# Two of four output-row blocks of a convolution's first pointwise product, computed by seven block products instead of eight at the turn between query groups of a Conformer layer

## The chip, the cores and the metric

The kernel runs on one core of one Trainium2 chip. The metric is the device time of one execution in microseconds (us); lower is better. Shown are the median of three runs, and one execution taken by the hardware profiler, from which all durations come.

## The reference

The reference is one Conformer layer on x of shape [2, 4000, 512] in bfloat16, with normalisations over the 512 features:

```python
x1 = x  + 0.5 * silu(ln(x) @ w_ff1_a) @ w_ff1_b           # 512 -> 2048 -> 512
x2 = x1 + softmax(q k^T * scale) v @ w_o                   # q, k, v from ln(x1)
h  = ln(x2) @ w_pw1                                        # 512 -> 1024
h  = h[..., :512] * sigmoid(h[..., 512:])                  # gate
dc = depthwise convolution of h over time, three taps      # then a norm over all tokens
x3 = x2 + silu(norm(dc)) @ w_pw2
x4 = x3 + 0.5 * silu(ln(x3) @ w_ff2_a) @ w_ff2_b
return ln(x4)
```

The change concerns `ln(x2) @ w_pw1` and the gate behind it.

## The kernel before

**Chunks and groups.** Each of the two sequences is cut into eight chunks of 512 tokens (the last has 416), so there are 16 chunks, c or t = 0 to 15. The first feed-forward part runs over all chunks, then the attention, then the second feed-forward part. The attention (`attention`, L2050) runs over 16 query groups g, one per chunk, and in each over 32 tiles of 128 keys; the loop variable is kt = 0 to 31, called a step of the group here. Chunk g - 1 passes beside group g through everything that follows its attention: `units_late` finishes its product with the values in steps 0 to 6 of group g, projects it, and normalises it (`ln_beside`, L1127, temporaries `ltm`, then transposes into `lnT[0]`). From `lnT[0]` comes the first pointwise product.

**Scores and values by seven products.** In groups 1 to 7 and 9 to 15 the scores of key tiles 2 to 29 are computed by quads of four key tiles (`score_quad`, L1993): 2 x 2 blocks of keys and of queries, seven block products instead of eight (the Strassen-Winograd scheme), every matmul with 256 columns (208 in the narrow groups). A quad takes four steps. It uses the PSUM banks s0 (called c), s1 (x) and s2 (h). Product 5 goes to h and is copied by ScalarE to `m5s` in SBUF (the tile region xt); product 1 goes to c and is copied to h; product 6 accumulates onto h; VectorE adds h and m5 into x; product 2 accumulates onto c, which is then done; product 7 accumulates onto h, and VectorE adds h and m5 into m5; products 3 and 4 accumulate onto x and h. Exponentials follow on ScalarE. Groups 0 and 8 ("plain") compute all scores directly. Key tiles 0, 1 and 30 are direct in every group, with four matmuls of 512 columns, in steps 0, 1 and 30. The tail of 32 keys is done by `tail_scores` (L2232) in step 24 (21 in group 0), in bank s1. The product with the values likewise takes seven products per pair of key tiles (`pv`), in banks y0 to y3 and s3, and is joined by VectorE in `pv_join` at the turn to the next group. The sums of the softmax (`pair_sums`, `sum_plain`, `sum_tail`, `split_sums`) are VectorE's too.

**The first pointwise product.** For chunk t, `pw1` (L2405) computes one block of 128 output rows by four matmuls of 512 columns. `conv_b` (L2361) takes a block of the gate's half and ScalarE computes its tanh into `th`; `conv_a` (L2372) takes the matching block of the other half and VectorE multiplies: (tanh + 1) times the PSUM bank, into `G`. A pair of the two, `pair(t, jj)` (L2733), serves block jj of four. Pairs 0 and 1 of chunk t come in steps 24 and 28 of group t + 1, in banks s0 and s1, and pairs 2 and 3 in steps 3 and 5 of group t + 2, in banks y1 and y3 (`att_hook`, L2741). Then GpSimd copies the one-column halos, and `taps_beside` (L2423) applies the three taps with ScalarE and VectorE.

**What sets the order.** The recorded operations are put in order by a planner (`Plan`, `once` at L272). It works from a table of instruction costs, moves matmuls ahead of each other within 8 us of the recorded order, and gives each engine its instructions in the order in which its model would start them; so a change moves neighbours too. SyncE issues nearly all DMAs in such an order: the streams of key and value forms (`kfd`, `v12d`), transposes, and stores. A DMA that waits at the head of the queue holds back what is behind it.

**Where things lie.** Region "work" holds `lnT[0]`, `lnT[1]` and `ltm`; `lnT[1]` also holds the next queries (`lin`), `last7` (L860), in which the last pair sums are kept, and the transposed sums `sT`. Region "wff" holds the weights `Wp1` and the gate's buffers. All recorded instructions carry line L93 in the profile, so operations are told apart by the regions they write and read, as in `s<-work,wff`: a PSUM bank s from work and wff.

Of the kernel before, what the change touches and what calls it, by code (L numbers as in the profile page):

```python
# [17 lines left out]
CHUNK = TPC * TILE  # L18
# [532 lines left out]
class Conformer:  # L551
# [35 lines left out]
    def memory(self):  # L587
# [269 lines left out]
        self.m3 = C.view(oP + (self.NP - 1) * 1024, CHUNK, parts=3)  # L857
        self.b_m3 = [C.buf("m3", oP + (self.NP - 1) * 1024 + j * 2 * TILE, 2 * TILE) for j in range(TPC)]

        self.last7, self.b_last7 = C.view(oLT + 4096, CHUNK), C.buf("last7", oLT + 4096, 2 * CHUNK)  # L860
        self.hl = C.view(oHL, 1024).rearrange("p (h c k) -> p h c k", h=2, c=DC)
        self.sT = C.view(oLT + 6144, 1024).rearrange("p (h c k) -> p h c k", h=2, c=DC)
        self.b_sT = [C.buf("sT", oLT + 6144 + h * 1024, 1024) for h in range(2)]
# [932 lines left out]
    def pair_sums(self, g, j, step):  # L1796

        S, s, W = self.S, g % TCB % 2, width(g)
        hw = W // 2
        i, n = self.group(j)[0], len(self.group(j))  # L1800
        r, m, ft, b_f = self.p_home(g, i)
        at = (i + 1) % 2
        R = self.Rt[:, r:r + n, :, 0:hw]
        a12, a22 = R[:, :, 0], R[:, :, 1]
        a11, a21 = [t[:, m:m + n, 0:hw] for t in self.Tt]
        b_11, b_21 = [b[m:m + n] for b in self.b_T]
        b_12, b_22 = self.b_R[r:r + n], self.b_R2[r:r + n]
        s4, s1, s2 = [ft[:, k, at:at + n, 0:hw] for k in range(3)]
        if step < 4:
            out, x, y, op, rd, wr = ((s1, a21, a22, ALU.add, b_21 + b_22, [b_f[1]]),  # L1810
                                     (s2, s1, a11, ALU.subtract, b_11 + [b_f[1]], [b_f[2]]),
                                     (a21, a11, a21, ALU.subtract, b_11 + b_21, b_21),
                                     (s4, a12, s2, ALU.subtract, b_12 + [b_f[2]], [b_f[0]]))[step]
            S.op("DVE", lambda e: e.tensor_tensor(out=out, in0=x, in1=y, op=op), reads=rd, writes=wr)
            return
        acc = self.acc[s][:, 0:W].rearrange("p (h k) -> p h k", h=2)
        if step == 6:
            S.op("DVE", lambda e: e.tensor_tensor(out=acc[:, 0], in0=acc[:, 0], in1=acc[:, 1], op=ALU.add),
                 reads=[self.b_acc[s]], writes=[self.b_acc[s]])
            return  # L1820
        if j == 0:
            return
        sig = [ft[:, 0:2, at + k, 0:hw] for k in range(n)]
        t, b_t = (self.P30, self.b_P30) if j < GROUPS - 1 else (self.last7, self.b_last7)
        two = t[:, 0:W].rearrange("p (h k) -> p h k", h=2)
        if step == 4:
            out, x, y, rd, wr = two, sig[0], sig[1], b_f[0:2], [b_t]
        elif j == 1:
            _, _, f0, b_0 = self.p_home(g, 0)
            out, x, y, rd, wr = acc, two, f0[:, 0:2, 1, 0:hw], [b_t] + b_0[0:2], [self.b_acc[s]]  # L1830
        else:
            out, x, y, rd, wr = acc, acc, two, [b_t, self.b_acc[s]], [self.b_acc[s]]
        S.op("DVE", lambda e: e.tensor_tensor(out=out, in0=x, in1=y, op=ALU.add), reads=rd, writes=wr)
# [216 lines left out]
    def attention(self, old, hook):  # L2050

        for g in range(NCK):
            W, plain = width(g), g % TCB == 0
            for kt in range(KT):
                if plain:
                    self.ring = [0, 1, 2]
                else:
                    self.ring, self.rings["S"] = list(self.ASIDE.get(kt, (0, 1))), 0
                if plain and kt < KT - 1 or kt < 2 or kt == KT - 2:
                    ps, b_ps = self.scores(g, kt, None if plain else self.bank((0, 2)[kt] if kt < 2 else 0))  # L2060
                    if kt < KT - 2:
                        self.exp_pair(g, kt, ps, b_ps)
                    else:
                        self.act(self.P30[:, 0:W], ps[:, 0:W], AF.Exp, [b_ps], [self.b_P30], scale=SCALE)
                elif not plain and kt < KT - 2:
                    self.score_quad(g, *divmod(kt - 2, 4))
                if g == 0 and kt < 2:
                    self.pop(old // 2 if kt == 0 else old - old // 2)
                if kt == (24 if g else 21):
                    self.tail_scores(g)  # L2070
                if g:
                    self.units_late(g - 1, kt)
                self.units(g, kt)
                self.next_queries(g, kt, 9 if g else 0)
                hook(g, kt)
                self.forms(g, kt)
                self.keys_swap(g, kt)
                self.tick()

    @staticmethod  # L2080
    def group(j):
# [150 lines left out]
    def tail_scores(self, g):  # L2232


        S, s, W = self.S, g % 2, width(g)
        n = W // 4
        ps, b_ps = self.bank(1)
        hT, b_hT = self.hT[TCB - 1][:, TPC - 1], self.b_hT[TCB - 1][TPC - 1]
        parts = [(slice(j * REST, (j + 1) * REST), slice(j * n, (j + 1) * n)) for j in range(4)]
        for cc in range(DC):  # L2240
            for j, (r, q) in enumerate(parts):
                self.mm(ps[r, 0:n], hT[:, cc, r], self.qT[s][:, cc, q], cc == 0, cc == DC - 1 and not self.any_score,
                        [b_hT, self.b_qT[s][cc]], b_ps, inc=cc == DC - 1 and j == 3, tile_position=(0, j * REST))
# [12 lines left out]
        S.dma("SP", k, *[lambda e, r=r: e.dma_start(self.ptail[r, 0:W].rearrange("p (j q) -> p j q", j=4), src)  # L2256
                         for r, q in parts], reads=[self.b_pqd], writes=[self.b_ptail])
# [210 lines left out]
    def fetch_conv(self, t):  # L2468
        W = width(t)
        self.load(self.dcv4[t][:, :, 0:W], self.dcvd[t].rearrange("p (c k) -> p c k", c=DC)[:, :, 0:W], self.b_dcv[t],  # L2470
                  reads=self.b_dcvd[t])

    def halo_left(self, t, jj):

# [154 lines left out]
    def program(self, any_score):  # L2629
# [163 lines left out]
        def gate(eng):  # L2793
            gates.pop(0)(eng)
# [232 lines left out]
```

## Time and profile before

| | us |
|---|---|
| median of three runs | 1882.87 (1882.72 to 1882.94) |
| the profiled execution's own time | 1882.47 |
| its span | 1878.7 |
| TensorE (PE) busy | 1860.1 |
| VectorE (DVE) busy | 1463.0 |
| ScalarE (ACT) busy | 1306.9 |
| GpSimd (POOL) busy | 133.2 |
| DMA, mean over the span | 123 GB/s |

The span is the time from the first to the last instruction in the profile. PE stands for matmuls, PEld for the weight loads ahead of them, which run beside the matmuls. A group of the attention lasts some 63 us. Group rows give: line, engine, operation, written and read regions, shapes and count, then busy us and mean ns, then idle time before them. Timeline rows give start, duration, engine, operation and how many equal instructions were merged.

### The profile page before, as it was taken

The page shows a single profiled execution, that of the slowest core. Times are in us where ns is not written, and L with a number is a line of the kernel's source. Part 1 is how long each engine was busy: PE and PEld are TensorE (multiplying, and loading weights), DVE is VectorE, ACT ScalarE, POOL GpSimd, SP SyncE. Part 2 cuts the span into 40 slices and gives each one's busy share as a digit, 9 for nine tenths or more (in the row PEclk, how much of TensorE's full clock was granted, in tenths as well). Part 3 has the DMA queues.
Part 4 walks back from the last instruction along what each step waited for, and adds up shares of the span by engine and source line. Part 5 has one row for each costly group of instructions (what it writes and reads, how often), then busy time and mean ns, then how long its engine had stood idle before and what let it go on. Part 6 is the DMA issues. An engine that isn't in the chain of part 4 may idle for free.

```text
span 1878.7 us, 39230 instructions
## 1 busy us (share of the span) xinstructions
PE 1860.1 (99%) x15389; PEld 1442.7 (77%) x15389; DVE 1463.0 (78%) x3191; ACT 1306.9 (70%) x2419; POOL 133.2 (7%) x301
## 2 busy tenths in 40 slices
PE   9999999999999999999999999999998999999998
PEld 5888888866777777777677777777774888888886
DVE  7888888868667777776777677768778888888885
ACT  5777777644667777677667677777668687777773
POOL 1000000000000000000000000000011000000000
PEclk9999999999999999999999999999999999999999
DMA  7323344197545555447944444444375222222111
GB/s 191 101 79 91 80 113 105 57 265 214 173 144 151 158 170 166 107 133 177 248 125 133 130 122 114 122 137 121 111 203 171 74 61 71 77 46 61 49 43 33
DMA packets 325014, 231.52 MB, mean 123 GB/s; under 512 B 204179, under 2 KB 295638, under 8 KB 324566
## 3 DMA queue, kind: packets, MB, share of 16 engines
q1 hardware_dynamic: 324294, 228.68, 44.4%
q8 instruction: 123, 2.02, 0.4%
q14 instruction: 69, 0.57, 0.1%
q10 hardware_dynamic: 528, 0.26, 0.0%
HBM read 128.44 MB, written 55.79 MB: 98 GB/s over the span
## 4 chain that ended last, share of the span: by engine, by line
PE 97%; DVE 1%; ACT 1%; DMA 0%; issue 0%; DVEq 0%; ACTq 0%
PE s L93 48%; PE y L93 48%; DVE work L93 1%; ACT work L93 0%; DMA xt<-v12d 0%; DVE wff L93 0%; DVE xt L93 0%; DVE s L93 0%; ACT sums L93 0%; DMA work<-work 0%; ACT wff L93 0%; ACT keys L93 0%; ACT s L93 0%; ACT xt L93 0%; ACT L93 0%
## 5 line engine op out<-in xcount | busy, mean ns | idle before, releaser
L93 ACT ACTIVATE sums<-s 128x512 bf16<-128x512 f32 (+2 forms) x494 | 288.2, 584 | 171.3 <-PE s L93 169.9
L93 ACT ACTIVATE keys<-s 128x512 bf16<-128x512 f32 (+2 forms) x284 | 165.6, 588 | 183.6 <-PE s L93 166.4
L93 DVE TENSOR_TENSOR sums<-sums 128x512 bf16<-128x512 bf16 (+3 forms) x528 | 195.4, 398 | 75.0 <-ACT sums L93 70.0
L93 PE MATMUL y<-work,keys 128*128 128x256 bf16 x1920 | 244.6, 273 | 0.0
L93 PE MATMUL s<-work,keys 128*128 128x256 bf16 (+5 forms) x1456 | 224.5, 292 | 0.0
L93 ACT ACTIVATE work<-xt,work 128x512 bf16<-128x512 bf16 x268 | 206.7, 785 | 7.8 <-DVE work L93 7.8
L93 PE MATMUL y<-wff,keys 128*128 128x256 bf16 (+3 forms) x1592 | 209.1, 276 | 0.1
L93 PEld LDWEIGHTS y<-work,keys 128*128 128x128 bf16 x1920 | 187.8, 98 | 25.1
L93 PE MATMUL y<-sums,keys 128*128 128x256 bf16 (+1 forms) x1440 | 202.6, 270 | 0.0
L93 PE MATMUL s<-sums 128*128 128x256 bf16 x1296 | 193.8, 273 | 0.0
L93 DVE TENSOR_TENSOR keys<-keys 128x1024 bf16<-128x1024 bf16 (+2 forms) x262 | 169.2, 662 | 28.8 <-ACT keys L93 13.6
L93 PE MATMUL y<-work,wff 128*128 128x256 bf16 (+2 forms) x1116 | 184.0, 292 | 0.0
L93 PEld LDWEIGHTS y<-wff,keys 128*128 128x128 bf16 (+1 forms) x1592 | 151.2, 98 | 32.4 <-issue 3.3
L93 DVE BATCH_NORM_STATS2 work<-xt 128x6 f32<-128x512 bf16 x251 | 163.9, 680 | 5.1 <-DMA xt<-in_x_dram 4.3
L93 PEld LDWEIGHTS s<-work,keys 128*128 128x128 bf16 (+1 forms) x1456 | 119.2, 97 | 50.6 <-ACT sums L93 4.0
L93 PEld LDWEIGHTS y<-sums,keys 128*128 128x128 bf16 x1440 | 138.8, 98 | 24.1 <-DVE sums L93 0.6
L93 POOL TENSOR_TENSOR work<-work 128x4 f32<-128x4 f32 (+3 forms) x107 | 89.8, 840 | 807.4 <-DVE work L93 804.9
L93 PE MATMUL s<-work,wff 128*128 128x512 bf16 (+5 forms) x668 | 141.0, 345 | 3.2 <-DVE work L93 2.7
L93 PEld LDWEIGHTS s<-sums 128*128 128x128 bf16 x1296 | 126.7, 98 | 20.0
L93 PE MATMUL s<-work 128*128 128x512 bf16 (+4 forms) x565 | 138.5, 375 | 3.0 <-DVE work L93 1.8
L93 PE MATMUL y<-sums,xt 128*128 128x256 bf16 (+1 forms) x960 | 139.4, 270 | 1.5 <-DVE sums L93 0.8
L93 PEld LDWEIGHTS y<-work,wff 128*128 128x128 bf16 x1116 | 108.2, 98 | 29.8
(143 smaller groups left out, 3202.2 us busy)
## 6 DMA issues: line engine op xcount, KB each, us to landing
xt<-kfd SPq DMA_DIRECT2D x98, 384.0 KB, 3.3
xt<-v12d SPq DMA_DIRECT2D x105, 256.0 KB, 2.9
xd<-xt SPq DMA_DIRECT2D x28, 512.0 KB, 3.1
xt<-xd SPq DMA_DIRECT2D x28, 512.0 KB, 4.3
out_dram<-xt SPq DMA_DIRECT2D x14, 512.0 KB, 3.0
xt<-in_x_dram SPq DMA_DIRECT2D x13, 512.0 KB, 4.0
dcvd<-wff SPq DMA_DIRECT2D x48, 128.0 KB, 2.1
keys<-dcvd SPq DMA_DIRECT2D x12, 512.0 KB, 4.3
```

Source lines behind the costliest of these rows:

```text
L93: return getattr(eng, self.name)(*self.args, **self.kw)
```

## The change

In thirteen chunks, t = 0 to 6 and 8 to 13 (`by_unit`), blocks 0 and 1 of both halves, that is four blocks of 128 rows, are no longer computed by `pw1` but by `gate_unit`. It works like a score quad: 2 x 2 blocks (rows: gate half and other half, 256 each; contraction: 2 x 256; columns: 2 x 256 tokens), seven products of four matmuls of 256 columns, in banks s0 to s2, with `m5s`. Its four steps come in steps 30 and 31 of group t + 1 and 0 and 1 of group t + 2, and for t = 6 the last three all in step 31. Pairs 2 and 3 of these chunks move to steps 24 and 28 of group t + 1.

The four weight sums are computed once in group 0 (`gate_weights`), stored to DRAM (`wpd`), and loaded into the place of `ltm` (`WS`, 512 KB) in step 22 of each group with a unit. The four token differences (`gate_tokens`, `TF`) are computed in steps 24 to 27 into the place of `lnT[1]`; so `last7` moves into the accumulator that is idle at the time. To leave bank s2 to the unit, the direct scores of steps 30 and 1 go to s1, and `tail_scores` goes to s0 behind the quad's step. `touch` writes the remaining columns of bank s1 where a narrow group uses it.

The diff, cut to its core:

```diff
-        self.last7, self.b_last7 = C.view(oLT + 4096, CHUNK), C.buf("last7", oLT + 4096, 2 * CHUNK)
+        self.last7 = [C.view(oACC + (1 - s) * 2048, CHUNK) for s in range(2)]
+        self.TF = [C.view(oLT + 4096 + m * 1024, 512).rearrange("p (t j k) -> p t j k", t=2, j=2) for m in range(4)]
+        self.WS = C.view(oLM, 2048).rearrange("p (m j d) -> p m j d", m=4, j=2)
+        self.wpd = nc.dram_tensor("wpd", [128, 2048], BF16, kind="Internal").ap()
+        self.th2 = W.view(24576, 2 * CHUNK, F32).rearrange("p (u k) -> p u k", u=2)
...
-        t, b_t = (self.P30, self.b_P30) if j < GROUPS - 1 else (self.last7, self.b_last7)
+        t, b_t = (self.P30, self.b_P30) if j < GROUPS - 1 else (self.last7[s], self.b_acc[1 - s])
...
-                    ps, b_ps = self.scores(g, kt, None if plain else self.bank((0, 2)[kt] if kt < 2 else 0))
+                    ps, b_ps = self.scores(g, kt, None if plain else self.bank(kt if kt < 2 else 1))
                     if kt < KT - 2:
                         self.exp_pair(g, kt, ps, b_ps)
                     else:
+                        self.touch(ps, b_ps, W)
                         self.act(self.P30[:, 0:W], ps[:, 0:W], AF.Exp, [b_ps], [self.b_P30], scale=SCALE)
                 elif not plain and kt < KT - 2:
                     self.score_quad(g, *divmod(kt - 2, 4))
+                self.unit_steps(g, kt)
+                if kt == (24 if g else 21):
+                    self.tail_scores(g)
                 if g == 0 and kt < 2:
                     self.pop(old // 2 if kt == 0 else old - old // 2)
-                if kt == (24 if g else 21):
-                    self.tail_scores(g)
...
+    def unit_steps(self, g, kt):
+        at = self.UNIT
+        if g == 0 and kt in (16, 18, 20, 22, 24):
+            self.gate_weights((kt - 16) // 2)
+        t = g - 1
+        if self.by_unit(t):
+            if kt == 22:
+                self.load(self.WS.rearrange("p m j d -> p (m j d)"), self.wpd, self.b_WS, reads=[self.b_wpd])
+            if 24 <= kt < 28:
+                self.gate_tokens(kt - 24)
+            for n, k in enumerate(at):
+                if k == kt or k > KT - 1 == kt and (g + 1) % TCB == 0:
+                    self.gate_unit(t, n)
+        t = g - 2
+        if self.by_unit(t) and g % TCB:
+            for n, k in enumerate(at):
+                if k - KT == kt:
+                    self.gate_unit(t, n)
+
+    UNIT = (30, 31, 32, 33)
...
-        ps, b_ps = self.bank(1)
+        ps, b_ps = self.bank(0 if g else 1)
...
+    def by_unit(t):
+        return 0 <= t < NCK - 2 and t % TCB != TCB - 1
+
+    def gate_weights(self, step):
...
+    def gate_tokens(self, step):
+        q = lambda e, k: self.lnT[0][:, 2 * k:2 * k + 2, 2 * e:2 * e + 2, :]
+        t1, t2, t4, t3 = self.TF
...
+    def gate_unit(self, t, step):
+        (c, b_c), (x, b_x), (h, b_h) = [(ps[:, 0:CHUNK], b) for ps, b in (self.bank(k) for k in range(3))]
+        m5, b_m5 = self.m5s, self.b_m5s
...
+        forms = {1: (raw(0, D), q(0, 0)), 2: (raw(1, D), q(1, 0)), 3: (sums(2), q(1, 1)), 4: (raw(1, 0), form(2)),
+                 5: (sums(0), form(0)), 6: (sums(1), form(1)), 7: (sums(3), form(3))}
+
+        def product(k, ps, b_ps, start=False):
+            (a, b_a), (m, b_m) = forms[k]
+            for u in range(2):
+                out = ps[:, u * 256:(u + 1) * 256].rearrange("p (t k) -> p t k", t=2)
+                for j in range(2):
+                    self.mm(out, a(u, j), m(j), start and u == 0 and j == 0, u == 1 and j == 1,
+                            [b_a] + b_m, b_ps, skip_group_check=True)
+
+        def plus(out, b_out):
+            S.op("DVE", lambda e: e.tensor_tensor(out=out, in0=h, in1=m5, op=ALU.add), reads=[b_h, b_m5], writes=[b_out])
...
+        def tanh(src, b_src, k):
+            self.act(half(k), two(src), AF.Tanh, [b_src], self.b_th, scale=0.5)
+
+        def gate(src, b_src, k):
+            wr = [b for jj in range(2) for b in (self.b_G[t % 2][jj], self.b_Gl[t % 2][jj], self.b_Gr[t % 2][jj])]
+            S.op("DVE", lambda e: e.scalar_tensor_tensor(
+                out=g[:, 0:2, 1 + k * 256:1 + (k + 1) * 256], in0=half(k), scalar=1.0, in1=two(src), op0=ALU.add, op1=ALU.mult),
+                reads=[b_src] + self.b_th, writes=wr)
+
+        if step == 0:
+            product(5, h, b_h, True)
+            self.act(m5, h, AF.Copy, [b_h], [b_m5])
+            product(1, c, b_c, True)
+            self.act(h, c, AF.Copy, [b_c], [b_h])
+        elif step == 1:
+            product(6, h, b_h)
+            plus(x, b_x)
+            product(2, c, b_c)
+            tanh(c, b_c, 0)
+        elif step == 2:
+            product(7, h, b_h)
+            plus(m5, b_m5)
+            product(3, x, b_x)
+            tanh(x, b_x, 1)
+            gate(m5, b_m5, 1)
+        else:
+            product(4, h, b_h)
+            gate(h, b_h, 0)
+            for jj in range(2):
+                self.halo_left(t, jj)
+                self.halo_right(t, jj)
+                if t:
+                    self.after(2 + 2 * jj, lambda jj=jj: self.taps_beside(t - 1, jj))
...
             if kt in here and (0 <= g - 1 < tail or g - 1 == tail and here.index(kt) < self.KEEP):
-                pair(g - 1, here.index(kt), self.bank(1) if kt == 24 else None)
-            if 0 <= g - 2 < tail and kt in there:
+                pair(g - 1, here.index(kt) + 2 * (not any_score and self.by_unit(g - 1)))
+            if 0 <= g - 2 < tail and kt in there and (any_score or not self.by_unit(g - 2)):
                 pair(g - 2, 2 + there.index(kt))
```

More of the change, by code (lines that the diff above doesn't have):

```diff
@@ L858, in memory @@
         self.b_m3 = [C.buf("m3", oP + (self.NP - 1) * 1024 + j * 2 * TILE, 2 * TILE) for j in range(TPC)]
-        self.last7, self.b_last7 = C.view(oLT + 4096, CHUNK), C.buf("last7", oLT + 4096, 2 * CHUNK)
+        self.last7 = [C.view(oACC + (1 - s) * 2048, CHUNK) for s in range(2)]
+        self.TF = [C.view(oLT + 4096 + m * 1024, 512).rearrange("p (t j k) -> p t j k", t=2, j=2) for m in range(4)]
+        self.b_TF = [C.buf("TF", oLT + 4096 + m * 1024, 1024) for m in range(4)]
+        self.WS = C.view(oLM, 2048).rearrange("p (m j d) -> p m j d", m=4, j=2)
+        self.b_WS = [C.buf("WS", oLM + m * 1024, 1024) for m in range(4)]
+        self.wpd = nc.dram_tensor("wpd", [128, 2048], BF16, kind="Internal").ap()
+        self.b_wpd = Buf("wpd")
+        self.th2 = W.view(24576, 2 * CHUNK, F32).rearrange("p (u k) -> p u k", u=2)
         self.hl = C.view(oHL, 1024).rearrange("p (h c k) -> p h c k", h=2, c=DC)
@@ L2471, in fetch_conv @@
                   reads=self.b_dcvd[t])
+    @staticmethod
+    def by_unit(t):
+        return 0 <= t < NCK - 2 and t % TCB != TCB - 1
+    def gate_weights(self, step):
+        S = self.S
+        if step == 4:
+            self.store(self.wpd, self.WS.rearrange("p m j d -> p (m j d)"), self.b_WS, [self.b_wpd])
+            return
+        a11, a12, a21, a22 = [self.Wp1[:, 2 * e:2 * e + 2, lo:lo + 256] for lo in (D, 0) for e in range(2)]
+        s1, s2, s4, s3 = [self.WS[:, m] for m in range(4)]
+        b1, b2, b4, b3 = [[b] for b in self.b_WS]
+        out, x, y, op, rd, wr = ((s1, a21, a22, ALU.add, [], b1), (s2, s1, a11, ALU.subtract, b1, b2),
+                                 (s4, a12, s2, ALU.subtract, b2, b4), (s3, a11, a21, ALU.subtract, [], b3))[step]
+        S.op("DVE", lambda e: e.tensor_tensor(out=out, in0=x, in1=y, op=op), reads=rd + [self.b_Wp1], writes=wr)
@@ new lines, in gate_tokens @@
+    def gate_tokens(self, step):
+        q = lambda e, k: self.lnT[0][:, 2 * k:2 * k + 2, 2 * e:2 * e + 2, :]
+        t1, t2, t4, t3 = self.TF
+        b1, b2, b4, b3 = [[b] for b in self.b_TF]
+        out, x, y, rd, wr = ((t1, q(0, 1), q(0, 0), [], b1), (t2, q(1, 1), t1, b1, b2), (t3, q(1, 1), q(0, 1), [], b3),
+                             (t4, q(1, 0), t2, b2, b4))[step]
+        self.S.op("DVE", lambda e: e.tensor_tensor(out=out, in0=x, in1=y, op=ALU.subtract),
+                  reads=rd + self.b_lnT[0], writes=wr)
@@ new lines, in gate_unit @@
+    def gate_unit(self, t, step):
+        S = self.S
+        (c, b_c), (x, b_x), (h, b_h) = [(ps[:, 0:CHUNK], b) for ps, b in (self.bank(k) for k in range(3))]
+        m5, b_m5 = self.m5s, self.b_m5s
+        raw = lambda e, lo: (lambda u, j: self.Wp1[:, 2 * e + j, lo + u * 128:lo + (u + 1) * 128], self.b_Wp1)
+        sums = lambda m: (lambda u, j: self.WS[:, m, j, u * 128:(u + 1) * 128], self.b_WS[m])
+        q = lambda e, k: (lambda j: self.lnT[0][:, 2 * k:2 * k + 2, 2 * e + j, :], self.b_lnT[0][2 * k:2 * k + 2])
+        form = lambda m: (lambda j: self.TF[m][:, :, j, :], [self.b_TF[m]])
+        forms = {1: (raw(0, D), q(0, 0)), 2: (raw(1, D), q(1, 0)), 3: (sums(2), q(1, 1)), 4: (raw(1, 0), form(2)),
[9 more added lines that the diff above has]
+            S.op("DVE", lambda e: e.tensor_tensor(out=out, in0=h, in1=m5, op=ALU.add), reads=[b_h, b_m5], writes=[b_out])
+        half = lambda k: self.th2[:, :, k * 256:(k + 1) * 256]
+        two = lambda ap: ap.rearrange("p (u k) -> p u k", u=2)
+        g = self.G[t % 2]
+        def tanh(src, b_src, k):
[29 more added lines that the diff above has]
+                    self.after(2 + 2 * jj, lambda jj=jj: self.taps_beside(t - 1, jj))
```

## The prediction

> **What bounds the kernel now.** First the page's head, its slices and its chain of what ended last.
>
> ```profile
> span 1878.7 us, 39230 instructions
> ...
> PE 1860.1 (99%) x15389; PEld 1442.7 (77%) x15389; DVE 1463.0 (78%) x3191; ACT 1306.9 (70%) x2419; POOL 133.2 (7%) x301
> ...
> PEclk9999999999999999999999999999999999999999
> ...
> PE 97%; DVE 1%; ACT 1%; DMA 0%; issue 0%; DVEq 0%; ACTq 0%
> ```
>
> TensorE (PE) is busy throughout, at the full granted clock, and is 97% of the chain that ended last. A busy figure alone does not show that nothing is left between matmuls, because ends are modelled. So I read the timeline of one stretch of attention for the pitch from start to start, where runs of equal matmuls follow each other:
>
> ```profile
> 712.89 1.47 PE L93 MATMUL y<-sums,keys 128*128 128x256 bf16 x12
> ...
> 714.20 0.60 PE L93 MATMUL s<-xt 128*128 128x256 bf16 x4
> ...
> 716.38 1.89 PE L93 MATMUL y<-work,wff 128*128 128x512 bf16 x8
> ...
> 718.11 0.60 PE L93 MATMUL s<-xt,keys 128*128 128x256 bf16 x4
> ```
>
> Twelve matmuls of 256 columns take 714.20 - 712.89 = 1.31 us, 109.2 ns each; eight of 512 columns, the kind that the change removes, take 718.11 - 716.38 = 1.73 us, 216.3 ns each. Twice the columns cost 1.98 times as much: narrow matmuls lose nearly nothing here. Third, what PE's weight loads waited for in 450 to 1400 us, the attention:
>
> ```profile
> PEld s L93 <- DVE s L93: 5.5, 12, 0.7
> PEld s L93 <- ACT sums L93: 4.4, 14, 0.4
> PEld s L93 <- DVE xt L93: 3.0, 5, 0.9
> ...
> PEld s L93 <- ACT s L93: 0.8, 3, 0.4
> ```
>
> These (total, times, longest) are the waits of the score quads, which work as the new unit will; small against 950 us. So a PE stream made shorter makes the attention shorter, unless the new waits take it back. Last, the other engines in twelve microseconds at three turns of groups, then in the rest of two groups (columns: stretch, length, then busy time and instructions by engine):
>
> ```profile
> 642.00:654.00 12.00, 12.00 (x96) 8.60 (x94) 11.68 (x27) 8.04 (x15) 0.65 (x2) 1.00 0.47 136
> 705.00:717.00 12.00, 12.00 (x95) 8.44 (x94) 11.62 (x27) 7.04 (x13) 0.43 (x2) 1.00 0.51 148
> 768.00:780.00 12.00, 12.00 (x97) 8.60 (x95) 11.01 (x26) 8.08 (x14) 0.66 (x2) 1.00 0.42 99
> ...
> 654.00:697.00 43.00, 43.00 (x347) 32.97 (x346) 30.51 (x71) 31.90 (x65) 2.72 (x9) 1.00 0.60 178
> 717.00:760.00 43.00, 43.00 (x346) 33.02 (x345) 30.23 (x68) 31.58 (x64) 2.70 (x9) 1.00 0.56 163
> ```
>
> VectorE (DVE, the third busy figure) is 70% busy in the groups but 92 to 97% at the turns, where the change puts its new work. That is the danger.
>
> **The change, part by part.** *Matmuls.* Thirteen chunks (0 to 6 and 8 to 13) change. In each, four column blocks of four 512-column matmuls (16) give way to seven products of four 256-column matmuls (28). The order of the built programs says the same: 208 fewer of 512 columns, 364 more of 256, and one more of 96 (a call of touch). By the pitches above: 208 x 216.3 ns = 45.0 us leave; 364 x 109.2 ns = 39.7 us and 0.04 us come. That is **5.2 us less**, 0.4 us per chunk, all on PE, which is the path.
>
> This needs weight loads to stay hidden. They average 98 ns (the groups by line), and the twelve matmuls above held a pitch of 109 ns with a load each, so 28 loads for 16 cost nothing while columns are 256 or more. A rule speaks against that. The Trainium skill, "TensorE: Matmul & The Clock Gate", section Back-to-back issue gap, says that the spacing in a stream with weight loads is set by both, about 81 ns at 128 columns and 131 ns at 512; on a line between the two, 98 ns at 256 would be an estimate from that page. By it a chunk would go from 16 x 131 = 2.1 us to 28 x 98 = 2.7 us, and the kernel would lose 8.4 us instead of gaining 5.2. The trace disagrees: 216 and 109 ns.
>
> *Waits on PE's path.* A unit is a quad's chain: products 5 and 1, two ScalarE (ACT) copies, product 6, a DVE sum, product 7, a sum, and so on in banks s0 to s2. For the stalls it brings, the nearest row is the quads' waits above: 13.7 us over 98 quads (the ACT copies into xt of their first step: 84 of 512 and 14 of 416 columns) are 0.14 us each, so at most 13 x 0.14 = 1.8 us. It is an upper end because a load stands one matmul ahead and part of its wait passes under the matmul before. The lower end is below nothing: the two block pairs that go had waits too; 0.5 us is left for those. I take +0.8, nearer the middle, since the built order puts other products between the steps as it does for the quads.
>
> *DVE.* Per chunk two sums of 512 from PSUM are added (0.69 us by the quads' rows), the two gates stay in number but move to the turn, and four bfloat16 differences of 512 are added before the turn (0.42 us by the row of the query differences). At the turn that is 4 x 0.69 = 2.8 us more DVE. But the unit's 28 x 0.109 = 3.1 us of PE now lie at the turn too: 11.5 of 12 us becomes about 14.2 of 15.1. The share is unchanged, so I take nothing beyond the 0.8 above. In the built order the last pair sums and a statistics instruction stand ahead of the unit's first sum; the late joins of y1 and y3, the sums of the last full key tile and of the tail, and a tap sum stand around its second sum and its gates; the joins of y2 and s3 queue behind the gates. PE needs those joins only where it starts anew in y2 and s3, and thirty matmuls of product 2 on y0 (3.3 us) and the next quad's first steps stand between. If that cover were gone, each DVE operation waited for would cost 0.69 us.
>
> *ACT.* Two copies of 0.59 us are added per chunk and two tanh move to the turn: 2.4 us on 8 of 12 busy, 10.4 of 15. Nothing, covered by ACT's idle third. What queues behind a late copy are exponentials of the next pair.
>
> *Moved blocks and banks.* Blocks 2 and 3 go from steps 3 and 5 to steps 24 and 28, and use s0 and s1. The tail scores now share s0 with the first of them, which therefore waits for their exponential (274 ns by its row); eight matmuls of 256 columns, 0.87 us, stand between in the built order. Nothing, and 0.2 us a chunk if that cover fails. Scores 30 and 1 go to s1 behind a gate or tanh that, placed by the rows' durations, ends 0.1 to 0.3 us before. The last pair sums' home moves into the idle accumulator: no cost.
>
> *DMA.* A load of 512 KB joins SyncE's (SP) queue in each of the thirteen, waiting for the four transposes out of the same buffer; one store in group 0. In the trace the last three transposes are issued over 688.27 to 693.13 us. With 2.5 us to landing the load can start near 695.6, holds the queue under half a microsecond and lands in some 4.3 us (the row of the 512 KB loads of x), near 700.4; its first use is product 5, about ten microseconds after the tail scores at 697.5. Queued behind are three stores that PE does not wait for, then loads of key and value forms, which stood at 696.5 and 703.3 before and can slip by a few tenths. Cover: seven microseconds. Without it one turn would wait up to that, and PE with it.
>
> *GpSimd (POOL).* The same halo copies, up to four a chunk behind the last gate instead of two and two, 0.26 us each, waited for only by the tap products some steps later. Nothing.
>
> *Once only.* Four weight sums of 0.42 us on DVE in group 0, where it has slack. At the turn into the plain group 8, the unit's last three steps share one step of the loop, so fewer products stand between: 0 to 1 us, inside the 0.8. Ahead of and behind the attention the matmuls stand in the same order as before.
>
> Sum: -5.2 + 0.8 = -4.4 us. The profiled execution took 1882.47 us, 3.8 around its span of 1878.7, and would become 1878.1; it lies 0.4 under the median of the runs, 1882.87, so for a median I forecast **1878.5 us**.
>
> **Rivals.** (a) *The gain goes into small waits.* A turn with DVE at 95% has no room for errors; if each unit pays 0.2 to 0.4 us (the longest single waits of the quads are 0.4 to 0.9), 2.6 to 5.2 us come back. The time is 1880.3 to 1882.9, and I set it at 1881.3. For it: the turn's DVE share, and that the built order leaves only a tenth or two between the end of a sum and the product waiting for it. Against: the quads live with the same margins at 0.14 us. (b) *DVE becomes the bound of the turn: slower.* The place is the sum between products 6 and 7. Once the late joins stand ahead of it, PE waits one whole DVE operation of 0.69 us: 13 x 0.69 = 9.0, less 5.2, is +3.8, 1886.7 us. It decides from 0.40 us exposed per turn. Against it: DVE grows no faster than PE there. (c) *Weight loads set the pitch.* If load and columns did not overlap, 28 x (98 + 109) against 16 x (98 + 216) ns would be +0.8 us a chunk, +10 us, 1893. The row of twelve denies it. The skill's page above would also end on this side. (d) *The change does not do what it says*: excluded by the counts.
>
> **How the numbers follow.** About 0.2%, 3.8 us, is what a measurement of this kernel can tell from no change. The forecast gets 0.59, its own range is 1876.9 (nothing lost, and 0.7 of old waits gone) to 1879.9 (1.8 and a little more); 0.55 of it is under 1879.1. Rival (a) gets 0.30, (b) 0.10, (c) 0.01. Faster by 0.2%: 0.55 plus 0.03 from the best of (a), 0.58; within: 0.31; slower: 0.11. The range for eight in ten runs from 1876.9 through all of (a), to 1882.9.
>
> **What would show it.** PE's 512-column rows lose 208 and the 256-column rows gain 364, at the same pitches: the 5.2. Waits of loads of bank s for DVE and ACT grow by no more than 2 us over the attention: the 0.8. DVE at the turns stays under 97% in stretches three microseconds longer; if the row DVE s or DVE xt grows by over 5 us, (a) or (b) is right. A wait on the load of work from wpd would make the DMA part wrong. A granted clock under 1.0 would make all of it wrong.

## The result and the profile after

The changed kernel takes 1895.36 us (median of five runs, 1891.93 to 1898.57) against 1882.87 (1882.28 to 1883.26) for the kernel before. The ratio is 1.0068, with a 95% interval of 1.0051 to 1.0084: about 12.8 us slower, where 4.4 us faster was forecast. Here and below a difference in us is the ratio times the time of the kernel before; it can be about 1 us from the difference of the two medians, which is 12.5 here. The profiled execution after took 1898.57 us, the longest of the five, and its span grew by 15.7 us.

The head and the chain from the page of the changed kernel:

```profile
span 1894.4 us, 39621 instructions
...
PE 1854.3 (98%) x15432; PEld 1457.4 (77%) x15546; DVE 1490.9 (79%) x3266; ACT 1321.2 (70%) x2452; POOL 134.5 (7%) x301
...
PE 89%; DVE 5%; ACT 3%; DMA 2%; issue 1%; DVEq 0%; SPq 0%; ACTq 0%
```

PE is busy for some microseconds less than before, and yet its share of the chain has fallen from 97% to 89%. What it lost has gone to DVE, ACT and DMA, so PE now waits. (The weight loads went from 15389 to 15546, which is the 364 - 208 + 1 of the plan; a hundred or so matmul records are missing from this trace, so its PE busy figure is rough.) What PE waited for, in the whole span of the changed kernel (total us, times, longest):

```profile
PE s L93 <- DVE s L93: 14.7, 16, 3.4
PE s L93 <- ACT sums L93: 4.0, 6, 1.1
PE s L93 <- DVE work L93: 3.4, 5, 1.2
...
PE y L93 <- DVE sums L93: 1.4, 4, 0.4
```

The same view of the kernel before:

```profile
PE s L93 <- DVE work L93: 4.4, 6, 1.2
PE s L93 <- DVE s L93: 2.3, 6, 0.4
...
PE y L93 <- DVE sums L93: 0.8, 2, 0.4
```

The row DVE s grew by 12.4 us, and ACT sums is new with 4.0. All rows of this view together went from 12.0 to 27.7 us. Behind the first stands a wait of DVE that the kernel before did not have (waits of DVE, changed kernel):

```profile
DVE work L93 <- DMA work<-work: 10.4, 9, 3.0
```

A DMA from work to work is a transpose into `lnT[0]`, and the DVE instruction that waits for it is the first token difference. One of the nine places, from the timeline of the changed kernel (start, duration, engine, operation, how many, and in brackets the idle time before it and what ended it):

```profile
563.68 4.87 SPq L93 DMA_TRANSPOSE work<-work  x3
...
569.92 0.43 DVE L93 TENSOR_TENSOR work<-work 128x512 bf16<-128x512 bf16 x1 [1.62 <-DMA work<-work]
570.27 0.42 DVE L93 TENSOR_TENSOR xt<-sums 128x512 bf16<-128x512 bf16 x1
570.60 0.42 DVE L93 TENSOR_TENSOR work<-work 128x512 bf16<-128x512 bf16 x1
570.94 0.69 DVE L93 TENSOR_TENSOR work<-work,xt 128x512 f32<-128x512 f32 x1
571.54 0.76 DVE L93 TENSOR_TENSOR work<-work 128x512 bf16<-128x512 bf16 x2
572.21 0.70 DVE L93 TENSOR_TENSOR s<-s,xt 128x512 f32<-128x512 f32 x1
572.96 0.61 PE L93 MATMUL s<-xt,keys 128*128 128x256 bf16 x4 [1.46 <-DVE s L93]
```

Read it from the bottom. PE stands 1.46 us before product 7 of a score quad, because the sum of that quad (`s<-s,xt`) starts only at 572.21. Ahead of that sum in DVE's queue stand all four differences (the rows `work<-work` in bfloat16), and ahead of these DVE has been idle for 1.62 us: the first difference needs the last of four transposes, which SyncE issues one behind the other until 568.55. The sum itself needs no transpose; it is merely queued behind an instruction that does. In the kernel before, the same sum and product stand like this:

```profile
568.50 0.70 DVE L93 TENSOR_TENSOR s<-s,xt 128x512 f32<-128x512 f32 x1 [1.02 <-PE s L93]
...
569.32 0.60 PE L93 MATMUL s<-xt,keys 128*128 128x256 bf16 x4
```

There DVE waited for PE, and PE for nothing. Across the groups there are ten such places in the changed kernel, all in the middle of the steps 22 to 24 and none at the turn; PE waits 12.7 us at them. In eight of the ten all four differences stand ahead of the sum, in two of them three. In one more group the four stand ahead of the sum too, but the first starts at 697.55 us without a wait for a transpose, and PE waits only 0.21 us there.

Behind two of them the granted clock falls: behind the longest, of 3.44 us, and the third longest, of 1.78 us; behind the second longest, of 1.92 us, it stays at 1.00. The stretches of 2 us around the longest (busy us and instructions of PE, PEld, DVE, ACT, POOL, then PEclk):

```profile
886.00:888.00 2.00, 1.48 (x16) 1.05 (x13) 0.00 (x0) 0.99 (x3) 0.00 (x0) 1.00 0.64 194
888.00:890.00 2.00, 0.00 (x0) 0.00 (x0) 1.86 (x6) 0.04 (x1) 0.00 (x0) 1.00 0.96 226
890.00:892.00 2.00, 1.07 (x7) 0.94 (x8) 0.96 (x4) 0.00 (x0) 0.00 (x0) 0.65 0.91 251
892.00:894.00 2.00, 2.00 (x26) 1.38 (x25) 0.76 (x2) 1.18 (x3) 0.00 (x0) 0.50 0.76 181
894.00:896.00 2.00, 2.00 (x13) 1.06 (x12) 1.81 (x6) 0.52 (x1) 0.00 (x0) 0.99 0.36 79
```

PE stood 3.44 us until 890.92, and from then to 894 it ran at half pace, which cost about another 1.5 us. The second dip, at 1210 to 1216 (0.87, 0.50 and 0.78 in three such stretches), cost about 1.7. So the balance is -5.2 for the matmuls, +15.7 for PE's waits and +3.2 for the clock, together +13.7 of the +15.7; 2.0 us are in no row.

### The profile page after: what moved, and what is told of

Read it like the earlier page. It is cut to its first block, busy times and chain, and to the rows that moved or that the text cites. A ratio compares the mean times of both kernels' runs of the same rounds, so it can differ in the third digit from the quotient of the medians.

```text
span 1894.4 us, 39621 instructions
## 1 busy us (share of the span) xinstructions
PE 1854.3 (98%) x15432; PEld 1457.4 (77%) x15546; DVE 1490.9 (79%) x3266; ACT 1321.2 (70%) x2452; POOL 134.5 (7%) x301
## 4 chain that ended last, share of the span: by engine, by line
PE 89%; DVE 5%; ACT 3%; DMA 2%; issue 1%; DVEq 0%; SPq 0%; ACTq 0%
PE s L93 46%; PE y L93 43%; DVE work L93 2%; DMA work<-work 2%; ACT work L93 1%; ACT sums L93 1%; DVE wff L93 1%; DVE s L93 1%; DVE sums L93 1%; DVE xt L93 1%; ACT wff L93 0%; ACT xt L93 0%; ACT keys L93 0%; ACT s L93 0%; DVE keys L93 0%
## 5 line engine op out<-in xcount | busy, mean ns | idle before, releaser
L93 PE MATMUL s<-work,keys 128*128 128x256 bf16 (+5 forms) x1429 | 219.6, 291 | 1.9 <-ACT sums L93 0.3
L93 PE MATMUL y<-wff,keys 128*128 128x256 bf16 (+2 forms) x1590 | 208.7, 276 | 1.2 <-DVE keys L93 0.8
L93 PE MATMUL y<-sums,keys 128*128 128x256 bf16 (+1 forms) x1440 | 207.3, 271 | 0.3
L93 PE MATMUL s<-work 128*128 128x512 bf16 (+4 forms) x721 | 157.7, 345 | 5.7 <-DVE work L93 1.8
L93 PE MATMUL s<-work,wff 128*128 128x512 bf16 (+5 forms) x808 | 156.8, 332 | 1.9 <-DVE work L93 1.6
L93 PE MATMUL s<-xt,keys 128*128 128x256 bf16 (+1 forms) x816 | 125.3, 272 | 14.9 <-DVE s L93 14.7
L93 PE MATMUL y<-work,wff 128*128 128x256 bf16 (+1 forms) x924 | 138.6, 273 | 0.0
```

The source lines that it names most:

```text
L93: return getattr(eng, self.name)(*self.args, **self.kw)
```

## The experiments

The theory after the traces: the term that failed is the four differences' wait for the transposes at the head of DVE's queue. The rivals: their work is too much for DVE (load, not wait); the unit's place at the turn costs by itself; or ScalarE's waits, the row ACT sums, are what matters. All ratios below are against runs of the kernel before on the same chip. Each edit also gives the planner another program to put in order, so neighbours move too; no experiment holds the rest of the order fixed.

**The differences held back.** The changed kernel, but the differences come a step later and are held behind the gate of block 2:

```diff
-            if 24 <= kt < 28:
-                self.gate_tokens(kt - 24)
+            if 25 <= kt < 29:
+                self.gate_tokens(kt - 25, self.b_G[t % 2][2])
...
-                  reads=rd + self.b_lnT[0], writes=wr)
+                  reads=rd + self.b_lnT[0] + [behind], writes=wr)
```

> The four token differences are recorded one step of the group later (25 to 28) and made to wait for the gate product of block 2, a VectorE instruction that itself follows matmuls that read the same transposed tokens. So they can't stand at the head of VectorE's queue while the transposes are under way. Theory A (VectorE waits in order on the transposes, and the sum that product 7 needs is queued behind): the ten waits of PE, 12.7 us in all, and the two dips of the clock behind the longest of them, some 3.4 us, go: 1879 to 1883 us, no VectorE wait of work on DMA work<-work over 0.3 us. Rival B (VectorE has too much to do at the turn itself, as in the prediction's rival (b)): the work at the turn grows, 1893 us or more. Rival C (ScalarE waits on the transposed sums, and the matmuls that covered it at steps 3 and 5 have gone): 1892 to 1895, since this does not touch it.

Measured: 1879.31 us (1878.24 to 1881.85) against 1884.66, ratio 0.9977 (0.9967 to 0.9986), 4.3 us faster. The row `DVE work <- DMA work<-work` is gone, and PE's waits for DVE s are nearly as before the change:

```profile
PE s L93 <- DVE s L93: 2.1, 6, 0.4
```

The same stretch of DVE's timeline:

```profile
568.53 0.70 DVE L93 TENSOR_TENSOR s<-s,xt 128x512 f32<-128x512 f32 x1 [1.02 <-PE s L93]
...
573.55 0.69 DVE L93 SCALAR_TENSOR_TENSOR wff<-wff,s 128x512 bf16<-128x512 f32 x1 [0.25 <-PE s L93]
574.15 0.42 DVE L93 TENSOR_TENSOR xt<-sums 128x512 bf16<-128x512 bf16 x1
574.49 0.42 DVE L93 TENSOR_TENSOR work<-work 128x512 bf16<-128x512 bf16 x1
```

The sum starts at 568.53, 0.03 us from where it stood before the change, and the first difference comes at 574.49, behind a gate, without waiting. The same instructions in another place turn 12.8 us of loss into a gain.

**The differences alone, in the kernel before.** No unit, no moved blocks; the four differences are computed in steps 24 to 27 and nobody reads them:

```diff
+                if 0 <= g - 1 < NCK - 2 and g % TCB and 24 <= kt < 28:
+                    self.gate_tokens(kt - 24)
```

> The kernel before, with the four token differences of steps 24 to 27 added and nothing else; nobody reads them, so the output is the reference's. Theory A: the wait comes with them: VectorE waits of work on DMA work<-work of about 1 us in most groups, and 5 to 14 us slower than before. Rival B: four operations of 0.42 us in a stretch where VectorE has slack, 0 to 1 us. Rival C: no change.

Measured: 1900.02 us (1897.09 to 1901.43), ratio 1.0079 (1.0062 to 1.0096), 14.9 us slower. Without any of the rest of the change the differences cost as much as the whole change: the two intervals overlap. DVE waits for the transposes again, and PE for DVE (the second row was 2.3 us in the kernel before):

```profile
DVE work L93 <- DMA work<-work: 7.3, 7, 2.1
```

```profile
PE s L93 <- DVE s L93: 8.4, 14, 1.6
```

**The same, held back.** The differences of the last kernel, held behind the gate of block 0:

```diff
-                if 0 <= g - 1 < NCK - 2 and g % TCB and 24 <= kt < 28:
-                    self.gate_tokens(kt - 24)
+                if 0 <= g - 1 < NCK - 2 and g % TCB and 25 <= kt < 29:
+                    self.gate_tokens(kt - 25, self.b_G[(g - 1) % 2][0])
```

> The kernel before with the same four token differences, now held behind the gate of block 0 of step 24, so that VectorE has the same work and no wait for the transposes. Theory A (the wait costs, not the work): at most 3 us over the kernel before. If the work itself is what costs: 10 us or more over it, as with the differences that wait.

Measured: 1883.47 us (1882.01 to 1884.85) against 1883.81, ratio 0.9995 (0.9985 to 1.0004). So 52 DVE instructions of 0.42 us, 22 us of work, cost nothing that can be measured where they do not wait. Load as such is excluded.

**The wait alone.** In place of the four differences, one DVE copy of two elements per partition that reads the same transposes:

```diff
+                if 0 <= g - 1 < NCK - 2 and g % TCB and kt == 24:
+                    self.look()
...
+    def look(self):
+        self.S.op("DVE", lambda e: e.tensor_copy(self.TF[0][:, 0, 0, 0:2], self.lnT[0][:, 3, 0, 0:2]),
+                  reads=self.b_lnT[0], writes=[self.b_TF[0]])
```

> The kernel before with one copy of two elements per partition on VectorE in step 24 of each group, which reads the transposed tokens and so waits for the transposes, and no token differences. Theory A: most of what the four differences cost, 5 to 15 us over the kernel before, with VectorE waiting on DMA work<-work. If the work is what costs: within 2 us of it.

Measured: 1891.38 us (1889.37 to 1894.03), ratio 1.0042 (1.0025 to 1.0059), 7.9 us slower. What DVE and PE waited for in it:

```profile
DVE work L93 <- DMA work<-work: 15.5, 13, 2.2
```

```profile
PE s L93 <- DVE s L93: 5.7, 12, 1.0
...
PE y L93 <- DVE sums L93: 2.3, 3, 1.5
```

An instruction with next to no work costs 8 us (4.7 to 11 by the interval) by waiting at the head of a queue. With the differences in its place PE's waits rise further, from 18.1 us in all to 27.2 (12.0 in the kernel before), and the time by another 7. That fits the differences themselves passing ahead of the sum behind the wait, three of the four at 505.92 us in that trace: work that is free elsewhere lengthens the stall here. This share was not separated from what else moved in the order.

**The unit without the differences.** The changed kernel with `gate_tokens` left out:

```diff
-            if 24 <= kt < 28:
-                self.gate_tokens(kt - 24)
...
-        form = lambda m: (lambda j: self.TF[m][:, :, j, :], [self.b_TF[m]])
+        form = lambda m: q(m % 2, m // 2)
```

> The changed kernel with the token differences left out: products 4 to 7 read plain blocks of the transposed tokens in their place, so half of the gated rows are not the reference's; all matmuls, sums and waits of the unit else stay. Theory A: 1877 to 1882 us, like the kernel with the differences held back or a little under it. Rival B: 1890 or more. Rival C: 1892 to 1895.

Measured: 1884.53 us (1883.87 to 1889.5), ratio 1.0004 (0.9995 to 1.0014): 11 us better than the change, but a miss, since the 5 us of the matmuls do not show. PE's waits in it:

```profile
PE s L93 <- DVE s L93: 4.7, 15, 0.5
...
PE s L93 <- ACT sums L93: 3.6, 6, 1.0
```

The 3.4 us waits are gone, the row ACT sums has stayed. That points at the second part. (The profiled execution took 1887.57 us, 3 above the median, and its granted clock was near 0.50 from some 1435 to 1442 us, behind the attention.)

**ScalarE's row sums held back.** ScalarE adds up the transposed softmax sums `sT` (in `sums_by_query`) about steps 5 to 6, and waits for their transposes there. Before the change it waited too, 16.0 us in all, but there the 16 wide matmuls of the pairs in steps 3 and 5 stood beside that wait. Here, in the changed kernel, these sums are held behind the exponential of quad 1; the differences stay as they are.

```diff
-                    self.sums_by_query(o % TCB % 2, 5)
+                    self.sums_by_query(o % TCB % 2, 6, o + 1)
...
+            late = []
+            if g is not None and g % TCB:
+                late = [self.b_T[0][self.p_home(g, 3)[1]]]
...
-                self.act(x, x, AF.Copy, self.b_sT, [self.b_sqs[s][ti]], accum_out=self.sq[s][:, ti:ti + 1])
+                self.act(x, x, AF.Copy, self.b_sT + late, [self.b_sqs[s][ti]], accum_out=self.sq[s][:, ti:ti + 1])
```

> The changed kernel with ScalarE's row sums of the transposed softmax sums held behind an exponential of the second quad, one step later, so that ScalarE does not wait on those transposes. Theory A: only the smaller part, PE's 3.7 us of waits for ScalarE in the first quads, goes: 1890 to 1894 us. Rival C (this is the main cause): 1884 or less. Rival B: no change, 1895.

Measured: 1893.97 us (1890.03 to 1896.8), ratio 1.0045 (1.0028 to 1.0062). PE's waits for ACT sums fall from 4.0 to 0.9 us and the kernel is some 4 us quicker than the change, though the two intervals overlap; its waits for DVE s stay at 13.6. So this is at most the smaller of two causes.

**Both held back.** The edits of the first and of the last kernel together.

> The changed kernel with the token differences held back behind the gate of block 2 and also ScalarE's row sums held back behind the second quad. If the ScalarE waits (PE on ACT sums, 2.0 us left with the differences held back) still cost something, 1 to 3 us under that kernel, a ratio to the kernel before of 0.996; if they are hidden, the same as it, 0.998.

Measured: 1877.25 us (1875.81 to 1881.31) against 1883.81, ratio 0.9969 (0.996 to 0.9979), 5.8 us faster, the best version of this study and ahead of both kernels. Its chain, and PE's waits in it:

```profile
PE 95%; DVE 2%; ACT 2%; issue 1%; DMA 0%; SPq 0%; DVEq 0%; ACTq 0%
```

```profile
PE s L93 <- DVE work L93: 4.1, 4, 1.3
PE s L93 <- DVE s L93: 2.7, 7, 0.6
```

**What the unit is worth by itself.** Two kernels: the unit without differences and with ScalarE's sums held back, and the kernel before with nothing but these sums held back (the diff of the sums above, applied to each).

> The changed kernel with gate_tokens left out (forms 4 to 7 read plain token blocks, so half the gated rows are not the reference's) and with ScalarE's row sums of the transposed softmax sums held behind the exponential of quad 1. It tells what kept the unit without the token differences at 1884.5 us instead of 1878. Theory (ScalarE's wait for the transposed sums took it, about 4 us of PE's waits on ACT sums, and nothing else of the unit costs): 1876 to 1880, ratio 0.996 to 0.998, PE's waits for ACT sums under 1 us. Rival (the unit's place at the turn costs by itself, as rival (a) of the prediction has it): 1882 to 1885, with PE's waits for DVE s over 4 us.

> The kernel before with only the row sums of the transposed softmax sums held behind the exponential of quad 1, nothing else changed. ScalarE waits there 16.0 us in all for the transposes, ten times. Theory (these waits cost only in the changed kernel, because the 16 wide matmuls of the pairs of steps 3 and 5 hide them before): 1883 to 1885, ratio 0.999 to 1.001. Rival (they cost the kernel before as well, and the version with both held back owes part of its gain to that and not to the unit): 1879 to 1882, ratio 0.997 to 0.9985.

Measured on the same chip: 1879.35 us (1878.45 to 1882.77), ratio 0.9972 (0.996 to 0.9984), and 1882.44 us (1881.72 to 1884.31), ratio 0.9988 (0.9979 to 0.9997), against 1884.80. The first kernel's waits of PE:

```profile
PE s L93 <- DVE s L93: 4.0, 12, 0.4
PE s L93 <- DVE work L93: 3.4, 5, 1.2
...
PE s L93 <- ACT sums L93: 0.6, 1, 0.6
```

With neither of the two waits the unit gains 5.3 us (3.0 to 7.5 by the interval) on the kernel before, and its rows of PE's waits sum to 13.0 us against 12.0: the unit's own stalls are small. But some 2.3 us are to be had in the kernel before as well by holding the sums back, between the two expectations. So what the unit adds to a kernel whose sums are held back is 1879.35 against 1882.44, some 3 us, and the intervals of these two just overlap; the first experiment, which leaves the sums alone, gives 4.3, and both held back against the second kernel here 3.6. The intervals do not tell these apart. They lie at or under the 4.4 of the forecast.

**The differences on GpSimd.** The changed kernel, with the four differences given to POOL, so that DVE's queue never waits for the transposes:

```diff
-        self.S.op("DVE", lambda e: e.tensor_tensor(out=out, in0=x, in1=y, op=ALU.subtract),
+        self.S.op("POOL", lambda e: e.tensor_tensor(out=out, in0=x, in1=y, op=ALU.subtract),
```

> The changed kernel with the token differences on GpSimd, which may wait for the transposes without holding VectorE. Theory A: 1876 to 1883 us, if GpSimd is done with the four in the seven or more microseconds before product 5. If GpSimd takes over 2 us for one of them, PE waits for it in products 5 to 7 and the time is above 1885.

Measured: 1899.44 us (1899.02 to 1900.0), ratio 1.008 (1.0063 to 1.0097), a miss: no better than the change. PE's waits for DVE s are down from 14.7 to 8.0 us, not to the 2.3 of the kernel before, and others rose. The worst place, from its timeline:

```profile
883.10 4.76 POOL L93 TENSOR_TENSOR work<-work 128x512 bf16<-128x512 bf16 x4 [12.73 <-PE s L93]
...
884.33 4.05 DVE L93 TENSOR_TENSOR sums<-sums 128x416 bf16<-128x416 bf16 x4 [0.68 <-ACT sums L93]
...
888.44 0.53 PE L93 MATMUL s<-sums,keys 128*128 128x208 bf16 x4 [1.93 <-DVE sums L93]
```

While POOL computes, DVE takes 4.05 us for four additions; in the unit without differences the mean of these additions (128x416, 56 of them) is 371 ns, 1.5 us for four. Rows of three DVE operations by line and shape (count, busy us, mean ns), first of this kernel:

```profile
L93 DVE TENSOR_TENSOR sums<-sums 128x512 bf16<-128x512 bf16 x408 | 163.1, 432 | 49.1 <-ACT sums L93 46.2
...
L93 DVE TENSOR_TENSOR work<-work,xt 128x512 f32<-128x512 f32 x84 | 64.6, 769 | 1.6
...
L93 DVE TENSOR_TENSOR xt<-sums 128x512 bf16<-128x512 bf16 x84 | 41.2, 490 | 13.2 <-PE y L93 12.1
```

and then of the unit without differences:

```profile
L93 DVE TENSOR_TENSOR sums<-sums 128x512 bf16<-128x512 bf16 x408 | 158.3, 420 | 54.1 <-ACT sums L93 51.4
...
L93 DVE TENSOR_TENSOR work<-work,xt 128x512 f32<-128x512 f32 x84 | 57.8, 688 | 1.5
...
L93 DVE TENSOR_TENSOR xt<-sums 128x512 bf16<-128x512 bf16 x84 | 35.4, 422 | 10.4 <-PE y L93 9.2
```

The three grew by 4.8 + 6.8 + 5.8 = 17.4 us. All three add two operands in SBUF. The Trainium skill, "GPSIMD Engine Reference", section Key points, says that GpSimd and VectorE share their interfaces to SBUF, and that there is contention when a VectorE instruction reads two operands from SBUF. The rows agree, and additions with one operand in PSUM did not grow: `s<-s,xt` of 512 columns took 67.5 us here and 67.8 there. On POOL itself one difference takes 1283 ns, three times DVE's 0.42 us. So one kind of wait was traded for another; how much of the 15 us is this contention alone was not separated.

## Why the prediction was wrong

**The step that failed** is the DVE part, where "four bfloat16 differences of 512 are added before the turn (0.42 us by the row of the query differences)" were costed by their duration and at nothing. Their work is indeed free where it does not wait (ratio 0.9995). But they read `lnT[0]`, and that they wait was not looked at, nor what is queued behind them. The prediction had the number: it worked out, for the load of the weight sums, that the last transposes are issued until 693.13 and land near 695.6. It used this for the DMA that overwrites their source and not for the DVE instructions that read their result. The built order, which the timeline above follows, has all four differences ahead of the sum of a quad that does not need them. In place of nothing the runs showed 7.9 us for the wait alone and 14.9 for the wait with the differences.

**The matmuls**, -5.2 us: right within what can be measured. The weight loads grew by the number foreseen, and the 256-column matmuls keep their pitch. Three neighbouring rows of the changed kernel's timeline:

```profile
568.27 0.60 PE L93 MATMUL y<-sums,keys 128*128 128x256 bf16 x4
568.71 0.60 PE L93 MATMUL s<-sums,keys 128*128 128x256 bf16 x4
569.15 0.60 PE L93 MATMUL y<-sums,keys 128*128 128x256 bf16 x4
```

Four of them start every 0.44 us, 110 ns each. The trace of the unit with neither wait (no differences, sums held back) has all its matmul records, as the trace before has, and the clock was 1.000 in both; PE is busy in it for 4.8 us less than the 1860.1 before:

```profile
PE 1855.3 (99%) x15546; PEld 1456.4 (78%) x15546; DVE 1472.8 (79%) x3215; ACT 1325.4 (71%) x2451; POOL 135.8 (7%) x301
```

Where the differences do not wait, the kernels with the whole change gain 4.3 and 5.8 us. Rival (c) is excluded with it: by the rule of the Trainium skill ("TensorE: Matmul & The Clock Gate", Back-to-back issue gap) these kernels would be 8.4 us slower than before, and they are faster. The rule does not hold for this stream.

**The waits on PE's path**, +0.8 us: right for the unit itself. With the two foreign waits away PE's waits sum to 13.0 us against 12.0. The row it was bounded from was misread, though: thirteen of the fourteen waits in `PEld s <- ACT sums`, 4.0 of its 4.4 us, are those of `tail_scores` (loads `s<-work,keys 128*32`), and the last is a load of 32 columns too, which no quad has. The quads' own rows sum to 9.3 us, under 0.10 a quad, so the upper end would have been 1.2 and not 1.8.

**DVE at the turn.** The forecast that its share stays under 97% holds for the change (14.40 of 15 us at 642 to 657) but was no test. In the version with both held back DVE is busy like this at two turns (columns as above):

```profile
642.00:654.00 12.00, 11.95 (x98) 8.75 (x98) 12.00 (x29) 8.94 (x17) 1.65 (x6) 1.00 0.30 83
705.00:717.00 12.00, 11.95 (x100) 9.03 (x100) 11.87 (x27) 9.32 (x17) 3.18 (x6) 1.00 0.44 131
```

DVE is full for twelve microseconds, PE does not wait, and this is the fastest kernel. A busy share at 100% is not yet a stall. Rival (b) ended on the right side and named the right queue, with the sum between products 6 and 7; but it placed it in the unit at the turn and gave load as the cause. The stall lies in a score quad of steps 22 to 24, ahead of the turn, and comes from a wait. Rival (a) is not seen either.

**ACT**, costed at nothing: wrong by a smaller amount. The prediction asked what the two tanh cost where they go to, not what the 16 wide matmuls of steps 3 and 5 had covered where they came from: ScalarE's wait for `sT`. PE's waits for ACT sums are 4.0 us. They are 2.0 to 4.0 us in each kernel here that has the blocks moved and the sums not held, and at most 0.3 in each that has the blocks in their old place. That the moved matmuls had covered them is argued from this; no run puts the matmuls back. Nor is the size firm: holding the sums back gained some 4 us in the changed kernel, 1.5 with the differences held back and 6 without differences, and only the last is clear of the intervals.

**DMA**, cover of seven microseconds for the load of the weight sums: no wait on it is seen. **The clock**: "a granted clock under 1.0 would make all of it wrong" was said as a condition from outside; it was 0.998 over the span of the profiled execution, in two dips right behind stalls. By itself it does not explain the loss: executions of the kernel before show 0.998 too, and the one execution of the changed kernel at 1.000 still took 1891.93 us. **The range** ended at 1882.9 because every bound was made for the unit; none was made for an instruction that stands elsewhere.

## What to carry to other kernels

Price a new instruction by what it waits for and by what is queued behind it on its engine, before its duration: here 22 us of DVE work were free in one place, and in another, behind a wait of a few tenths to 3 us and ahead of an urgent sum, cost 15 (the wait alone 8). When work is moved away, ask what wait of another engine it had covered in its old place. If an early instruction has a late reader, hold it behind something that is itself late; the unit then gained 3 to 4 us of the 5.2 that its matmul count says.

## What the runs showed of the hardware that was not expected

- A stall of PE can cost more than its length. After PE had stood for 3.44 us the granted clock was 0.50 for some 3 us, about 1.5 us more. The Trainium skill, "TensorE: Matmul & The Clock Gate", section The HAM clock gate, says that the clock falls to 4/8 after an idle window of about 3.4 us; that agrees here, where the slices place the fall some 3.1 us after PE had stopped. The second dip does not: PE had stood for only 1.78 us, after six microseconds of full work, and the clock fell some 1.4 us after PE had begun again. A wait of 1.92 us at 508.69 us had no dip behind it. What tells these two apart was not found.
- DVE additions of two SBUF operands slow down while GpSimd computes: four of 416 columns took 4.05 us beside 4.76 us of POOL work, and 1.5 us by the mean without it.
- A wait at the head of DVE's queue reaches PE through instructions that do not need what is waited for. The two-element copy made DVE idle for 15.5 us in all, in thirteen places; PE's waits grew by 6.1 us and the kernel by 7.9, about half of that idle time.
